# Three pairs of blocks chosen early in a kernel of attention, mixture of experts and feed-forward

## The chip, the cores and the metric

One NeuronCore of a Trainium2 chip runs the whole computation in one launch. The metric is the device time of one execution in microseconds (us); a kernel's time is the median of its runs. Profiles are of one execution, on the same core.

## The reference

```python
def reference(q, k, v, w_gate, w1, w2, w_in, w_out, alpha):       # cut to what matters
    # attention in chunks of 64: q, k, v are (8, 8, 576, 64)
    s = matmul(q_c, k_c.T) / 8
    p = exp(s - max(s)); p /= sum(p) + 1e-9
    x = matmul(p, v_c)                        # tokens x features: 4608 x 512
    # mixture of experts: 8 experts, each token goes to its best one
    logits = x @ w_gate                       # 4608 x 8
    e = argmax(logits); g = softmax(logits)[e]
    y[e == i] = g * (relu(x[e == i] @ w1[i]) @ w2[i])     # 512 -> 1024 -> 512
    # feed-forward: 512 -> 2048 -> 512
    h = y @ w_in
    return (max(h, 0) + alpha * min(h, 0)) @ w_out
```

`w_in` and `w_out` arrive as 64-bit numbers. Every product of the experts and of the feed-forward is made of three products of rounded parts (high x high, high x low, low x high).

## The kernel before, in words

**Attention and routing** goes over 36 tiles of 128 tokens. `STEP` is a hand-written order: in step s each named piece runs for the tile that lies its lag behind. Every few tiles `choose`, `rank` and `count` decide the expert of each token and its place among that expert's tokens; `place` writes the token's number into a table (PSUM tile `tb`) with one column for each block of 128 tokens of an expert. After 24 tiles (`TE`), `choose_early` takes the expert that has most tokens, and `begin_first` (L1029) copies the table and gathers this expert's first 384 tokens (`gather_first`), so that a first group of three tiles can go through its expert (`lead_up`, `lead_act`, `lead_down`) while the routing of the last tiles ends. `TAIL` is the written order of this change-over. In it, `slots` computes on DVE from the final counts which block each of 24 slots takes (16 pairs of 128-token blocks, 8 single blocks), where each result row goes (`yidx`) and the expert of each slot (`bx`); `end_table` copies the finished table, and `gather0` has POOL gather the first slot's rows by indirect DMA. `add_slots` hands the slots' experts to `Stream`, which loads expert weights in pieces of 512 KB on SP's queue (L428, L431), two ahead; each piece is split into a rounded part `whi` on ACT (L443) and the rest `wlo` (L451) on DVE, every fourth on POOL.

**Experts and feed-forward** run side by side (`experts_and_ffn`). The feed-forward goes over 12 groups of 384 tokens, each in 16 blocks f: an `fh` product (L340 to L342), `leaky` on DVE (L1206, L1207), the split of the result, an `fo` product (L385 to L387). The experts' work is 160 steps: 8 for each pair slot, 4 for each single slot; a step k is `slot_up` (`mh`), `act` (`mact`), its split and `slot_down` of the step before (`mo`). When a slot's last step is reached, the next slot's rows are turned (`take`: four transposes, into the bank `tr` and, for the second tile, into `mh`, which `act` must have read), the slot after is gathered on POOL, and in the step that follows `slot_out` scales the two accumulators on ACT (`row`), copies the row numbers on POOL and scatters the rows into `y_sorted` by an indirect DMA on POOL. Groups of the feed-forward read `y_sorted` in order, four blocks before they begin.

A planner (`due`, `pace`, `target`) says how many steps lie beside each block: straight lines through corners, of which the first is (block 1, 0 steps), the second (16, `FRONT`), and the others say when a group's rows must exist (`surely_done`). The order of the pieces within a block and its first step is `STEP2` in group 0, `STEP4` after it, `STEP3` for single slots; further steps of the same block (in group 0) run only the list's expert entries and its `("conv", "too")` entries.

**The conversion** of `w_in` and `w_out` from 64 bits (`Float64Weights`, L186 to L283) has 32 pieces; 12 are done beside the attention, 20 beside group 0, four ticks each: `bits` and `round` (L243, L244 on DVE, L254 on ACT, L255 on POOL), `square` (L261, ACT), `mask` (L269, DVE), `finish` (L282 on ACT, L283 on POOL). They share one buffer `word`. STEP2 has four ticks, two of them "too".

All of it is one order written out by hand: each engine takes its instructions in program order.

## Time and profile before

| | us |
|---|---|
| median of three runs (lowest, highest) | 1544.39 (1543.96, 1548.34) |
| the profiled execution | 1545.0 |
| its span, first to last instruction | 1543.2 |
| PE busy (matmuls) | 1475.8 |
| DVE / ACT / POOL busy | 834.1 / 660.8 / 451.9 |
| mean granted TensorE clock | 0.989 |

The span is the time between the first and the last instruction of the profiled execution; 1.8 us lie around it. PE is busy 96% of it, so a change is worth what it takes from the other 4%, from the stretches at the lower clock, or from PE's work. A share of the whole span hides where these are; the rows further down are therefore by stage.

### The profile page before, as it was taken

To read this page: it belongs to the slowest core of one execution; us is meant where nothing else is said; L and a number is where in the kernel's file an instruction comes from. 1 tells how busy PE (TensorE), PEld (TensorE's weight loads), DVE (VectorE), ACT (ScalarE), POOL (GpSimd) and SP (SyncE) were. 2 spreads that over 40 slices of the span, in tenths; PEclk is the share of its full clock that TensorE was granted. 3 is DMA by queue.
4 is the path that set the end of the run, shared out by engine and by line. 5 is a ranking of instruction groups with operands and counts; after the bars stand their busy time and mean duration, and the time that the engine had idled before them with its cause. 6 is when DMAs were issued, how large, how long until landed. Compare 5 with 4: busy or idle time off the path is not lost.

```text
span 1543.2 us, 25420 instructions
## 1 busy us (share of the span) xinstructions
PE 1475.8 (96%) x9736; PEld 1313.8 (85%) x9736; DVE 834.1 (54%) x1485; ACT 660.8 (43%) x1365; POOL 451.9 (29%) x428
## 2 busy tenths in 40 slices
PE   7887879988999999999999999999999999999998
PEld 5665768878899999999999999999989998999887
DVE  5688868776444444444444444444445555555343
ACT  6887446555423333333333333334334444344211
POOL 2256546666212212221232222212204223231100
PEclk9999899999999999999999999999999999999999
DMA  9998335555323323332342333233324544454000
GB/s 288 321 314 272 104 110 171 172 190 170 103 83 119 97 85 106 100 97 92 105 126 85 100 93 113 84 101 103 92 87 158 152 156 149 143 165 139 28 21 21
DMA packets 119128, 201.23 MB, mean 130 GB/s; under 512 B 12704, under 2 KB 63904, under 8 KB 119008
## 3 DMA queue, kind: packets, MB, share of 16 engines
q1 hardware_dynamic: 108112, 168.32, 35.1%
q0 software_dynamic: 10896, 31.31, 5.9%
q8 instruction: 76, 1.25, 0.3%
q14 instruction: 44, 0.36, 0.1%
HBM read 170.13 MB, written 29.46 MB: 129 GB/s over the span
## 4 chain that ended last, share of the span: by engine, by line
PE 77%; DVE 8%; DMA 6%; POOL 3%; issue 3%; ACT 1%; SPq 0%; POOLq 0%; another core or an unknown queue 0%; ACTq 0%; DVEq 0%
PE fh L340 8%; PE fh L342 8%; PE fh L341 8%; PE fo L385 8%; PE fo L386 8%; PE fo L387 8%; PE mh L342 3%; PE mh L341 3%; PE mh L340 3%; PE mo L385 3%; PE mo L387 3%; PE mo L386 3%; DMA kbd<-in_kh 2%; DVE word L269 2%; PE tr L304 2%
## 5 line engine op out<-in xcount | busy, mean ns | idle before, releaser
L451 DVE TENSOR_TENSOR wlo<-raw,whi 128x1024 fp32r<-128x1024 f32 x146 | 182.3, 1253 | 169.2 <-ACT whi L443 166.2
L340 PE MATMUL fh<-fxh,w 128*128 128x384 f32 x760 | 257.1, 338 | 6.1 <-DVE fact L1207 4.7
L443 ACT CAST whi<-raw 128x1024 fp32r<-128x1024 f32 x200 | 208.7, 1049 | 119.5 <-PE mo L387 49.7
L342 PE MATMUL fh<-fxh,w 128*128 128x384 f32 x760 | 257.0, 338 | 0.0
L341 PE MATMUL fh<-fxl,w 128*128 128x384 f32 x760 | 256.2, 337 | 0.3 <-issue 0.3
L451 POOL TENSOR_TENSOR wlo<-raw,whi 128x1024 fp32r<-128x1024 f32 x54 | 129.8, 2403 | 431.1 <-ACT whi L443 430.7
L1206 DVE TENSOR_SCALAR fact<-fh,alpha 128x384 f32<-128x384 f32 x190 | 116.9, 615 | 234.2 <-PE fh L342 226.9
L385 PE MATMUL fo<-w,fgh 128*128 128x512 f32 x567 | 225.1, 397 | 0.0
L386 PE MATMUL fo<-w,fgh 128*128 128x512 f32 x567 | 222.7, 393 | 0.0
L387 PE MATMUL fo<-w,fgl 128*128 128x512 f32 x567 | 221.8, 391 | 0.0
L1139 ACT ACTIVATE mact<-mh 128x256 f32<-128x256 f32 x160 | 61.2, 382 | 288.6 <-PE mh L342 287.0
L321 ACT CAST fgh<-fact 128x384 fp32r<-128x384 f32 x197 | 100.9, 512 | 180.8 <-DVE fact L1207 180.5
L340 PEld LDWEIGHTS fh<-fxh,w 128*128 128x128 f32 x760 | 143.5, 189 | 15.0 <-DVE fact L1207 5.6
L341 PEld LDWEIGHTS fh<-fxl,w 128*128 128x128 f32 x760 | 143.3, 189 | 8.2 <-issue 0.5
L342 PE MATMUL mh<-mxh,wlo 128*128 128x256 f32 x512 | 144.6, 282 | 0.0
L341 PE MATMUL mh<-mxl,whi 128*128 128x256 f32 x512 | 144.4, 282 | 0.0
L340 PE MATMUL mh<-mxh,whi 128*128 128x256 f32 x512 | 144.1, 282 | 0.0
L342 PEld LDWEIGHTS fh<-fxh,w 128*128 128x128 f32 x760 | 143.2, 188 | 0.0
L327 DVE TENSOR_TENSOR fgl<-fact,fgh 128x384 fp32r<-128x384 f32 x197 | 114.0, 579 | 35.6 <-ACT fgh L321 35.3
L327 DVE TENSOR_TENSOR mgl<-mact,mgh 128x256 fp32r<-128x256 f32 x128 | 63.0, 492 | 121.2 <-ACT mgh L321 121.2
L387 PEld LDWEIGHTS fo<-w,fgl 128*128 128x128 f32 x567 | 106.5, 188 | 23.4
L385 PEld LDWEIGHTS fo<-w,fgh 128*128 128x128 f32 x567 | 107.0, 189 | 17.5 <-ACT orow L1199 0.2
(231 smaller groups left out, 2702.8 us busy)
## 6 DMA issues: line engine op xcount, KB each, us to landing
raw<-in_w SPq DMA_DIRECT2D x200, 512.0 KB
vt<-in_vh SPq DMA_DIRECT2D x18, 520.0 KB
qt<-in_qh SPq DMA_DIRECT2D x18, 512.0 KB
kbd<-in_kh SPq DMA_DIRECT2D x36, 256.0 KB
x_tok<-x SPq DMA_DIRECT2D x36, 256.0 KB
x<-y_sorted SPq DMA_DIRECT2D x33, 258.0 KB
raw<-in_w_in SPq DMA_DIRECT2D x16, 512.0 KB
raw<-in_w_out SPq DMA_DIRECT2D x16, 512.0 KB
```

The source lines that it names most:

```text
L321: self.nc.scalar.copy(gh, self.g[key])
L327: self.nc.vector.tensor_sub(gl, t, gh.bitcast(F32))
L340: nc.tensor.matmul(b, wh[:, c, :], hi[:, c, :], start=(c == 0), stop=False)
L341: nc.tensor.matmul(b, wh[:, c, :], lo[:, c, :], start=False, stop=False)
L342: nc.tensor.matmul(b, wl[:, c, :], hi[:, c, :], start=False, stop=(c == 3))
L385: nc.tensor.matmul(o, gh[:, s], wh, start=first, stop=False)
L386: nc.tensor.matmul(o, gh[:, s], wl, start=False, stop=False)
L387: nc.tensor.matmul(o, gl[:, s], wh, start=False, stop=last)
L443: self.nc.scalar.copy(hi, raw)
L451: (engine or (self.nc.gpsimd if n % 4 == 3 else self.nc.vector)).tensor_sub(lo, raw, hi.bitcast(F32))
L1139: nc.scalar.activation(t, b, AF.Relu)
L1206: nc.vector.tensor_scalar(t, b, 0.0, s_.alpha[:, f:f + 1], op0=ALU.min, op1=ALU.mult)
```

## The change

- After 24 tiles `choose_pairs` computes on DVE, from the counts so far, three pairs of full blocks (256 tokens of one expert each; `NE` = 3), besides the early group: 18 small instructions, a prefix sum over the experts' full pairs among them. They become slots 0 to 2. `slots` deals out the rest only (`NL` = 21 slots).
- `gather0` moves from the end of `TAIL` to its beginning; the experts of the three pairs are given to `Stream` in `begin_first`, so that its loads go on without a stop, and `add_slots` has none to start.
- The rows of slots 0 to 2 have known places: `slot_out` writes them with a plain DMA on SP's queue instead of a scatter on POOL.
- `FRONT` rises from 30 to 40.
- In `STEP2` the second transpose comes after `down` instead of after the first, both `out` stand together, the gather and `take_low` move; in `STEP4` one entry moves.
- The pools of the second part, and the two PSUM pools of the lead group, are opened with `reuse_waits="tile"`: a tile waits for what lay in its own place, and not for all that lay in the place of its pool.
- The conversion loads its 13th piece at the start of the second part, no longer in the attention.

```diff
-FRONT = 30
+NE = 3
+NL = NS - NE
+AHEAD = GW + NE * PAIR
+FRONT = 40
 STEP2 = (
...
-    ("moe", "take", 0), ("moe", "take", 1), ("ffn", "in_high", 0), ("ffn", "high", 0), ("ffn", "in", 1),
-    ("moe", "act", 0), ("moe", "take_high", 0), ("moe", "down", 0), ("ffn", "in_low", 0), ("moe", "gather", 0),
-    ("moe", "out", 0), ("ffn", "in", 2), ("ffn", "low", 0), ("conv", "too", 0), ("ffn", "in_high", 1),
-    ("moe", "take_low", 0), ("moe", "high", 0), ("moe", "low", 0), ("moe", "split_high", 0), ("ffn", "in_high", 2),
-    ("conv", "", 0), ("conv", "too", 0), ("ffn", "down", 0), ("moe", "out", 1), ("ffn", "out", 2),
-    ("moe", "split_low", 0), ("moe", "take_high", 1), ("moe", "take_low", 1), ("ffn", "in_low", 2),
+    ("moe", "take", 0), ("ffn", "in_high", 0), ("ffn", "high", 0), ("ffn", "in", 1),
+    ("moe", "act", 0), ("moe", "take_high", 0), ("moe", "down", 0), ("moe", "take", 1), ("ffn", "in_low", 0),
+    ("moe", "out", 0), ("moe", "out", 1), ("ffn", "in", 2), ("moe", "take_high", 1), ("moe", "gather", 0),
+    ("moe", "take_low", 0), ("moe", "take_low", 1), ("ffn", "low", 0), ("conv", "too", 0), ("ffn", "in_high", 1),
+    ("moe", "high", 0), ("moe", "low", 0), ("moe", "split_high", 0), ("ffn", "in_high", 2),
+    ("conv", "", 0), ("conv", "too", 0), ("ffn", "down", 0), ("ffn", "out", 2),
+    ("moe", "split_low", 0), ("ffn", "in_low", 2),
...
 TAIL = (
     ("sum_logits", 30), ("transpose_x", 32), ("split_high", 0), ("gate", 27), ("weigh", 34), ("keep_x", 32),
+    ("gather0", 0),
...
-    ("place", 34), ("place", 35), ("down", 6), ("end_table", 0), ("low", 7), ("gather0", 0), ("down", 7), ("scale", 0),
+    ("place", 34), ("place", 35), ("down", 6), ("end_table", 0), ("low", 7), ("down", 7), ("scale", 0),
...
+    def choose_pairs(t1):
+        cnt = run[t1].rearrange("p a e -> p (a e)")
+        left, fi = small.tile([P, E], I32, tag="left", name="left"), small.tile([P, E], I32, tag="fi", name="fi")
+        nc.vector.scalar_tensor_tensor(left, early_oh, -float(GW), cnt, op0=ALU.mult, op1=ALU.add)
+        nc.vector.tensor_single_scalar(fi, left, 8, op=ALU.arith_shift_right)
...
+        nc.vector.tensor_copy(s_.pairs, val)
+        nc.vector.scalar_tensor_tensor(early_col, early_n, 2.0, early_col, op0=ALU.mult, op1=ALU.add)
...
     def more_psum(_):
         att.close()
-        lead.ps_h = ctx.enter_context(tc.tile_pool(name="ps_h1", bufs=1, space=PSUM))
-        lead.ps_o = ctx.enter_context(tc.tile_pool(name="ps_o1", bufs=1, space=PSUM))
+        own = dict(bufs=1, space=PSUM, reuse_waits="tile")
+        lead.ps_h = ctx.enter_context(tc.tile_pool(name="ps_h1", **own))
+        lead.ps_o = ctx.enter_context(tc.tile_pool(name="ps_o1", **own))
...
         gather_first()
+        choose_pairs(TE)
+        for a in range(NE):
+            stream.add(s_.pairs[a:a + 1, 1:2])
...
     def add_slots(_):
-        for i in range(NS):
+        for i in range(NL):
             stream.add(s_.bx[0:1, 1, i:i + 1])
-        for _ in range(RAWS):
-            stream.load()
...
-                        if stage == "mask" and s + 3 > NT:
+                        if stage == "bits" and s + 3 >= NT:
                             conv.leave()
...
-    conv.hold(ctx.enter_context(tc.tile_pool(name="c_held", bufs=1)))
-    two = ctx.enter_context(tc.tile_pool(name="c_two", bufs=2))
-    ps_m = ctx.enter_context(tc.tile_pool(name="ps_m", bufs=1, space=PSUM))
-    ps_f = ctx.enter_context(tc.tile_pool(name="ps_f", bufs=1, space=PSUM))
+    conv.hold(ctx.enter_context(tc.tile_pool(name="c_held", bufs=1, reuse_waits="tile")))
+    two = ctx.enter_context(tc.tile_pool(name="c_two", bufs=2, reuse_waits="tile"))
+    ps_m = ctx.enter_context(tc.tile_pool(name="ps_m", bufs=1, space=PSUM, reuse_waits="tile"))
+    ps_f = ctx.enter_context(tc.tile_pool(name="ps_f", bufs=1, space=PSUM, reuse_waits="tile"))
...
-        nc.gpsimd.indirect_dma_start(
-            out=y_sorted, out_offset=bass.IndirectOffsetOnAxis(ap=s_.yidx[:, a, i:i + 1], axis=0),
-            in_=row, in_offset=None,
-        )
+        if a < NE:
+            r = GW + a * PAIR + i * P
+            nc.sync.dma_start(y_sorted[r:r + P, :], row)
+        else:
+            nc.gpsimd.indirect_dma_start(
+                out=y_sorted, out_offset=bass.IndirectOffsetOnAxis(ap=s_.yidx[:, a - NE, i:i + 1], axis=0),
+                in_=row, in_offset=None,
+            )
```

## Rows read from the trace of the kernel before

**Rows 1.** Windows by stage: stretch, length, busy us per engine (count), PEclk, DMA share, GB/s.
```profile
218.00:375.00 157.00, 140.83 (x777) 124.69 (x778) 117.22 (x156) 93.00 (x166) 99.27 (x74) 0.96 0.54 177
375.00:1470.00 1095.00, 1092.43 (x6161) 993.86 (x6159) 528.60 (x809) 411.17 (x725) 251.73 (x254) 1.00 0.35 110
```

**Rows 2.** Waits of PE, 217 to 400 us: in total, times, longest.
```profile
PE tr L304 <- ACT mact L1139: 8.5, 3, 2.9
PE mo L385 <- ACT row L1166: 3.3, 3, 1.2
```

**Rows 3.** Timeline, DVE: start, us, engine, line, operation, tiles, count, [idle before <- releaser].
```profile
296.08 0.43 DVE L243 TENSOR_SCALAR word<-raw 128x512 int32<-128x512 int32 x1
...
302.10 0.43 DVE L243 TENSOR_SCALAR word<-raw 128x512 int32<-128x512 int32 x1 [1.20 <-POOL w L283]
```

**Rows 4.** Timeline, first `bits` and last subtraction of the 20 pieces.
```profile
222.65 0.42 DVE L243 TENSOR_SCALAR word<-raw 128x512 int32<-128x512 int32 x1
...
372.93 1.35 POOL L283 TENSOR_TENSOR w<-word,w 128x512 fp32r<-128x512 f32 x1
```

**Rows 5.** Timeline around the gather of a slot: POOL and ACT.
```profile
266.26 0.18 POOL L496 COPY ix<-table 128x2 int32 x1
...
267.07 0.62 ACT L282 CAST w<-word 128x512 fp32r<-128x512 f32 x1 [0.35 <-DVE word L269]
...
272.44 1.31 POOL L283 TENSOR_TENSOR w<-word,w 128x512 fp32r<-128x512 f32 x1
```

**Rows 6.** Timeline, the same DVE link alone and beside a weight split on POOL.
```profile
266.35 0.69 DVE L269 SCALAR_TENSOR_TENSOR word<-raw,word 128x512 f32<-128x512 f32 x1 [1.19 <-POOL word L255]
...
284.05 2.41 POOL L451 TENSOR_TENSOR wlo<-raw,whi 128x1024 fp32r<-128x1024 f32 x1
...
284.13 2.88 DVE L269 SCALAR_TENSOR_TENSOR word<-raw,word 128x512 f32<-128x512 f32 x1 [1.05 <-POOL word L255]
```

**Rows 7.** Timeline of PE: starts of one block's `fo`, a step, `fh`, the next step.
```profile
227.97 0.40 PE L385 MATMUL fo<-w,fgh 128*128 128x512 f32 x1
...
230.04 0.28 PE L340 MATMUL mh<-mxh,whi 128*128 128x256 f32 x1
...
232.86 0.33 PE L340 MATMUL fh<-fxh,w 128*128 128x384 f32 x1
...
234.96 0.28 PE L340 MATMUL mh<-mxh,whi 128*128 128x256 f32 x1
```

**Rows 8.** Timeline around the second scatter of a slot: DVE and POOL.
```profile
280.25 0.69 DVE L244 SCALAR_TENSOR_TENSOR word<-raw,word 128x512 int32<-128x512 int32 x1
...
281.75 1.01 POOL L1168 DMA_INDIRECT y_sorted<-row,yidx  x1 [1.86 <-ACT raw L261]
```

**Rows 9.** Timeline of the change-over to group 0: ACT and PE.
```profile
211.46 2.05 ACT L1072 ACTIVATE x<-fo,gfirst 128x512 f32<-128x512 f32 x3 [1.99 <-PE fo L387]
...
213.56 0.66 PE L304 MATMUL fi<-ident,x 128*128 128x128 f32 x4 [0.78 <-ACT x L1072]
...
217.82 0.44 PE L340 MATMUL fh<-fxh,w 128*128 128x384 f32 x1 [1.40 <-ACT fxh L308]
```

**Rows 10.** Timeline, DVE: one small instruction of `slots`.
```profile
190.46 0.17 DVE L923 SCALAR_TENSOR_TENSOR sl_single<-sl_over,sl_single 128x8 f32<-128x8 f32 x1
```

**Rows 11.** Timeline, DVE, the end of the attention.
```profile
153.93 0.17 DVE L712 TENSOR_SCALAR den<-av 128x8 f32<-128x8 f32 x1 [2.66 <-remote]
```

**Rows 12.** Timeline: the first weight split on POOL, PE's first product with it.
```profile
160.93 2.40 POOL L451 TENSOR_TENSOR wlo<-raw,whi 128x1024 fp32r<-128x1024 f32 x1
...
169.95 0.53 PE L340 MATMUL fh<-fxh,whi 128*128 128x384 f32 x1
```

**Rows 13.** Timeline, PE: second block of group 1.
```profile
400.59 0.44 PE L340 MATMUL fh<-fxh,w 128*128 128x384 f32 x1 [1.30 <-DVE fact L1207]
```

**Rows 14.** Timeline, DVE and POOL, of another piece.
```profile
289.24 0.41 DVE L243 TENSOR_SCALAR word<-raw 128x512 int32<-128x512 int32 x1
...
290.62 2.09 POOL L255 TENSOR_TENSOR word<-word,raw 128x512 int32<-128x512 int32 x1 [1.57 <-DVE word L244]
```

More of the change, by code (lines that the diff above doesn't have):

```diff
@@ L135, in surely_done @@
 def surely_done(n):
-    low = N
-    for full in range((N - GW) // PAIR + 1):
-        rest = N - GW - full * PAIR
+    if n <= NE:
+        return GW + n * PAIR
+    low, n, pairs = N, n - NE, NP - NE
+    for full in range((N - AHEAD) // PAIR + 1):
+        rest = N - AHEAD - full * PAIR
         for part in range(E + 1):
@@ L143, in surely_done @@
                     continue
-                over = max(0, full + part - NP)
-                m = min(max(min(n, NP) - full, 0), part - over)
+                over = max(0, full + part - pairs)
+                m = min(max(min(n, pairs) - full, 0), part - over)
                 done = PAIR * min(n, full)
@@ L148, in surely_done @@
                     done += max((P + 1) * m, rest - (PAIR - 1) * (part - m) - P * single)
-                if n >= NP:
-                    done = max(done, N - GW - P * max(0, single + 2 * over - (n - NP)))
-                low = min(low, GW + done)
+                if n >= pairs:
+                    done = max(done, N - AHEAD - P * max(0, single + 2 * over - (n - pairs)))
+                low = min(low, AHEAD + done)
     return low
@@ L483, with __init__ @@
 class Gather:
-    def __init__(self, nc, pool, table, slots, x_tok, g_tok):
-        self.nc, self.pool, self.table, self.slots, self.x_tok, self.g_tok = nc, pool, table, slots, x_tok, g_tok
+    def __init__(self, nc, pool, table, early, slots, x_tok, g_tok):
+        self.nc, self.pool, self.table, self.early, self.slots = nc, pool, table, early, slots
+        self.x_tok, self.g_tok = x_tok, g_tok
         self.xs, self.gs, self.rows = {}, {}, {}
@@ L493, in __call__ @@
         nc, n = self.nc, tiles_of(a)
-        r = nc.gpsimd.value_load(self.slots[0:1, 0, a:a + 1], min_val=0, max_val=NCODE - 2)
+        first = self.early[a:a + 1, 0:1] if a < NE else self.slots[0:1, 0, a - NE:a - NE + 1]
+        x_tok, g_tok = ((y[:TE * P] if a < NE else y) for y in (self.x_tok, self.g_tok))
+        r = nc.gpsimd.value_load(first, min_val=0, max_val=NCODE - 2)
         ix = self.pool.tile([P, 2], I32, tag="ix", name="ix", bufs=4)
@@ L501, in __call__ @@
             nc.gpsimd.indirect_dma_start(
-                out=x, out_offset=None, in_=self.x_tok,
+                out=x, out_offset=None, in_=x_tok,
                 in_offset=bass.IndirectOffsetOnAxis(ap=ix[:, i:i + 1], axis=0),
@@ L541, in tile_attention_moe_ffn @@
     s.table = const.tile([P, NCODE], I32, name="table")
-    s.yidx = const.tile([P, NS, 2], I32, name="yidx")
-    s.bx = const.tile([P, 2, NS], I32, name="bx")
+    s.yidx = const.tile([P, NL, 2], I32, name="yidx")
+    s.bx = const.tile([P, 2, NL], I32, name="bx")
     s.first = const.tile([P, GT], I32, name="first")
-    s.gather = Gather(nc, share, s.table, s.bx, s.x_tok, s.g_tok)
+    s.pairs = const.tile([P, 2], I32, name="pairs")
+    s.gather = Gather(nc, share, s.table, s.pairs, s.bx, s.x_tok, s.g_tok)
     s.early_i = const.tile([P, 2], I32, name="early_i")
@@ L638, in attention_and_routing @@
     nc.vector.tensor_scalar_mul(kmaxe, iota_f[:, :E], float(KMAX))
-    oneE = one.tile([P, NS], F32, name="oneE")
+    oneE = one.tile([P, NL], F32, name="oneE")
     nc.vector.memset(oneE, 1.0)
@@ L652, in attention_and_routing @@
     early_oh = one.tile([P, E], F32, name="early_oh")
+    early_n = one.tile([P, E], F32, name="early_n")
+    early_col = one.tile([P, E], F32, name="early_col")
     tb = ps_tb.tile([P, NCODE], F32, name="tb")
@@ L900, in slots @@
         ci, fi, ri = new([E], "ci", I32), new([E], "fi", I32), new([E], "ri", I32)
-        nc.vector.scalar_tensor_tensor(ci, early_oh, -float(GW), cnt, op0=ALU.mult, op1=ALU.add)
+        left = new([E], "left")
+        nc.vector.scalar_tensor_tensor(left, early_oh, -float(GW), cnt, op0=ALU.mult, op1=ALU.add)
+        nc.vector.scalar_tensor_tensor(ci, early_n, -float(PAIR), left, op0=ALU.mult, op1=ALU.add)
         nc.vector.tensor_single_scalar(fi, ci, 8, op=ALU.arith_shift_right)
@@ L917, in slots @@
         over = new([E], "over")
-        nc.vector.scalar_tensor_tensor(over, lo[:, 1], float(NP), part, op0=ALU.is_ge, op1=ALU.mult)
+        nc.vector.scalar_tensor_tensor(over, lo[:, 1], float(NP - NE), part, op0=ALU.is_ge, op1=ALU.mult)
         nc.vector.tensor_add(hi[:, 1], lo[:, 1], part)
@@ L1310, in experts_and_ffn @@
     ctx.enter_context(convs)
-    conv.use(convs.enter_context(tc.tile_pool(name="c_conv", bufs=1)), 2)
+    conv.use(convs.enter_context(tc.tile_pool(name="c_conv", bufs=1, reuse_waits="tile")), 2)
     first = dict(
```

46 lines of the change are left out of this document (32 added, 14 removed).

## The prediction

> **What bounds the kernel now.** I read the windows by stage first: where is TensorE idle? In 375 to 1470 us it works 1092 of 1095 us at full clock [rows 1], so work moved out of there is worth its own length and nothing more. Idle time lies in the attention, in the change-over after it and in 218 to 375, where the first group of the second layer runs beside the conversion of the last 20 of its 32 weight pieces: there PE is busy 140.8 of 157 us at a mean granted clock of 0.96, so 16.2 us idle, and 2 x 0.04 x 157 = 12.6 us at 1.2 instead of 2.4 GHz, worth 6.3 us.
>
> The waits of PE in that stage name the obvious suspect: the second transpose of a slot's rows waits three times, 8.5 us in all, for `mact`, and the first product of a new slot 3.3 us for the copy of the old accumulators [rows 2]. The reorder of STEP2 is about just these.
>
> But a wait of PE is worth its length only if PE is what ends last there. So the third view is the chain of one converted piece over DVE, ACT and POOL: `bits` (L243) starts at 296.08, and the next piece's at 302.10, having waited 1.20 us for the last subtraction of the piece before on POOL (L283) [rows 3]. The one buffer `word` makes the pieces strictly serial, 6.0 us each when nothing intervenes. The first starts at 222.65, the 20th ends at 372.93 + 1.35 = 374.28 [rows 4]: 151.6 us, back to back. 20 x 6.0 is 120; the rest is what POOL does between two links: a slot's gather holds it from 266.26 until L283 can start at 272.44, though ACT's link before that ended at 267.07 + 0.62 = 267.69, 4.7 us (three times, 14) [rows 5]; a weight split on POOL makes the next DVE link 2.88 instead of 0.69 us (six times, 13) [rows 6]; and the scatters come on top. **The conversion chain, not PE, sets the length of this stage**; PE's waits are where its slack shows.
>
> **The change, part by part.** Part 1, *40 steps instead of 30 beside group 0*. The planner's first corner moves from 30 to 40 steps at block 16; no later due is steeper, so the rest still runs to 137 steps at block 139 and 161 at 171. Blocks 1 to 15 now take 2, 3, 3 steps in turn instead of 2. Each block ticks the conversion 4 times and each step beyond its first twice more, as before. The 80 ticks (20 pieces x 4) end in the first pass of block 13 before, and after in that of block 11 (4 in block 0, then 6 + 8 + 8 in turn: 76 after block 10). What PE gets done by then: a step is 232.86 - 230.04 = 2.82 us, an `fh` 234.96 - 232.86 = 2.10, an `fo` 230.04 - 227.97 = 2.07 [rows 7]. Before: 2.1 + 13 x 4.17 + 25 x 2.82 + 3 slots' transposes of 1.0 = 129.8. After: 2.1 + 11 x 4.17 + 27 x 2.82 + 3.0 = 127.1. So if the chain's length stays, **2.7 us more** PE work is left when it ends. The ten steps themselves cost nothing: they leave a stage where PE is full. Ranges: 0 to +4.
>
> Part 2, *scatters of the first three slots from POOL to SP*. The second scatter of a slot starts at 281.75, after 1.86 us of waiting, and keeps POOL until 282.76; the chain's next POOL link had its input from L244's end at 280.94 and would start some 0.2 us later [rows 8]: 1.6 us lost. The second slot shows the same, the third scatters when the conversion is over: together **-3.2 us** of the chain. On SP the row copies stand behind nothing of the chain; queued behind them are the next weight loads, which are there a piece ahead, so I put them at 0, up to +1 per slot if they come late. Range -3.2 to +2.
>
> Part 3, *transposes and copies in another order*. By the waits it is worth 8.5 + 3.3 us and their share of the clock; in a stage set by the chain it is worth **0**, if no link of the chain waits for these PE instructions. The only one that could is the gather, which reuses the transposed rows' buffers: POOL goes into it at 266.26 straight from work, with no idle time named [rows 5]. What is late next is the chain.
>
> Part 4, *waits by tile instead of by pool*. Of three `scale` copies (211.46 to 213.51) the first transpose needs only the first, but starts at 213.56, after the third, and group 0 at 217.82 [rows 9]; the accumulators lie in pools that it must see emptied as a whole. By tile it starts when PE is done with `fo`, about 212.8; then ACT's five casts of 0.59 us follow `scale` without a hole (213.5 + 5 x 0.59 = 216.4) and group 0 starts there: **-1.4 us**; range -1.4 to 0.
>
> Part 5, *choosing the pairs, and gather0 early*. 18 small DVE instructions at 0.17 us, as one of their kind in `slots` [rows 10]: 3.1 us, at about 146 to 150 us. There DVE stands still for 2.66 us shortly after [rows 11], waiting for PE; what held PE the rows don't show. If that wait is tied to a time, it covers 2.7 of the 3.1; if to PE's own place in its order, nothing. gather0 holds POOL some 6.2 us as in [rows 5], ahead of the first weight split, which ran from 160.93 for 2.40 us; PE's first product with it is at 169.95 [rows 12]. Put back by the whole 6.2 the split ends at 169.5: covered, barely. The split's place also decides which DVE instruction it blocks, for 2.2 us either way [rows 6]. A conversion piece of 512 KB is no longer loaded there. Ends: -2.2, and 3.1 + 2.2 = +5.3; I take **+1.0**, toward the covered end, as DVE's idle row is the nearest. After the change gather0 no longer follows the table at the end of the change-over, but no wait there names it [rows 9].
>
> Part 6, *the steps' new rhythm later*. A group whose first block has no step waits 1.30 us for `fact` [rows 13], as group 1 does, and group 11 like it. By the new slope group 6 also begins with no step: **+1.3**. `slots` changes by single small instructions: 0.
>
> Sum: +2.7 - 3.2 + 0 - 1.4 + 1.0 + 1.3 = **+0.4 us**. The profiled execution took 1545.0 us (span 1543.2), the median of the runs is 1544.39; the difference applied to the median is **1544.8**. The parts' ends, not all at once, give 1538 to 1550 for this case.
>
> **A rule weighed.** When POOL's `wlo` starts at 284.05, the DVE link that starts at 284.13 takes 2.88 instead of 0.69 us [rows 6]. The Trainium skill's page "SBUF — State Buffer", section "SBUF: two separate sides", says why: the port pair that DVE and GpSimd share is an exclusive lock held for a whole instruction, so that the other fully blocks. The trace agrees: the split takes 2.41 of those 2.88. By this rule the two engines' idle shares are no room for ten steps; were they independent, PE's idle time could be filled and the sum would be rival A's. In the windows DVE and POOL together are busy 117.2 + 99.3 us in 157 [rows 1], stalls included.
>
> **Rivals.** *A: PE's waits are a loss of their own.* Then 8.5 + 3.3 us go, and three quarters of the clock's 6.3 (one of four falls at the stage's start): 16.5, less about 1 us that each of now five slots may still wait, plus parts 4 to 6 (+0.9): -10.6, **1534**. For it: PE waits just there. Against: the 20 pieces stand back to back, and their length is told by DVE's and POOL's own work.
> *B: the chain gets longer.* With three steps in a row, splits and copies of two steps lie between pairs of ticks. The piece whose `bits` is at 289.24, with POOL's add drawn out to 2.09 us, already takes until 296.08, 6.8 instead of 6.0 us [rows 3, 14]. If twelve of 20 pieces become such, 12 x 0.8 = 9.6, on top of the +0.4: **1554**. It decides against the kernel where the mean of an undisturbed piece passes 6.4 us. For it: DVE and POOL share the stage's work with little room. Against: there are hardly more steps to a tick, 8 to 22 against 2 to 6.
> *C: choose_pairs and gather0 aren't covered*: part 5 at its upper end, 4.3 more than taken, **1549**, at the edge of what counts as no change.
>
> **How the numbers follow.** About 0.3% (4.6 us) is what a measurement of this kernel can tell from no change. Forecast 0.42, A 0.29, B 0.20, C 0.09. Same: the forecast less its fringes of 0.03 and 0.01, and over half of C, 0.43; faster: A and the fringe, 0.32; slower: B, the rest of C and the fringe, 0.25. Cases of both signs hold much: the range reaches into both, **1532 to 1554**; the forecast's own is 1538 to 1550.
>
> **What would show it.** The `tr` waits on `mact` shrink in the profile after; if the stage from 218 us to the end of the 20th piece is nevertheless 147 to 149 us long, with PE idle near 20, part 3 is right at 0. No `y_sorted` on POOL before the fourth slot; the first `fi` before 213 us less the attention's shift; one more 1.3 us wait on `fact` near group 6. I am wrong if pieces no longer follow each other without gaps (then PE sets the stage, A), or if their mean rises (B).

## The result: 1560.0 us, slower by one per cent

The changed kernel takes 1560.03 us (median of five runs, 1557.19 to 1565.92) against 1544.39; the ratio is 1.010, 95% interval 1.0078 to 1.0123. A second series of the same program gave 1560.01 (1.0078 to 1.0122). Forecast were 1544.8, 1532 to 1554: the time lies above the range. The profiled execution took 1557.75 us, its span is 1555.9 (before: 1543.2).

The windows by stage, as in [rows 1], first the change-over, then group 0 with the conversion (columns: stretch, its length, busy us and count per engine, PEclk, DMA share, GB/s):

```profile
145.00:155.00 10.00, 5.44 (x50) 4.54 (x50) 7.46 (x36) 4.98 (x14) 8.11 (x9) 0.66 0.63 210
155.00:165.00 10.00, 5.01 (x97) 3.52 (x98) 5.30 (x13) 2.41 (x5) 7.76 (x8) 0.99 0.42 130
165.00:175.00 10.00, 6.12 (x32) 4.44 (x32) 8.40 (x23) 3.65 (x7) 3.97 (x4) 0.50 0.36 109
...
218.00:375.00 157.00, 138.43 (x774) 118.16 (x775) 119.19 (x156) 96.73 (x172) 99.42 (x72) 0.99 0.55 182
```

Group 0 looks as forecast: PE is idle 18.6 of 157 us (16.2 in [rows 1]), at a clock of 0.99 instead of 0.96. The change-over from 145 to 175 us does not: PE works 16.6 of 30 us (before 19.7), and at 1.2 GHz through all of the third line. PE's waits show the same, and a third place (line waited for, us in total, times, longest). First the change-over, 143 to 222 us, then group 0 (218 to 435), then all behind it:

```profile
PE bx L741 <- DVE lg_all L783: 3.8, 1, 3.8
PE lgt L777 <- DVE rk L839: 3.7, 1, 3.7
...
PE mo L394 <- ACT mgh L330: 5.1, 5, 1.9
PE mo L396 <- DVE mgl L336: 4.8, 12, 0.8
PE mh L349 <- ACT mact L1185: 4.0, 7, 1.5
...
PE mo L395 <- POOL wlo L460: 1.6, 3, 0.5
...
PE fh L349 <- DVE fact L1257: 3.2, 3, 1.3
PE tr L313 <- DVE fxl L321: 2.5, 1, 2.5
```

The waits of `tr` on `mact` (8.5 us) and of `mo` on `row` (3.3 us) of [rows 2] are gone. In their place PE waits some 15 us for `mgh`, `mgl`, `mact` and `wlo` (with 30 steps in the new order, 5.8 for `mgh` alone), and behind group 0 there is a new wait of 2.5 us, of `tr` on `fxl`.

To see where the time goes, I cut each trace at marks that every version has: the end of attention's last score products; ACT's first `scale` copy (`x<-fo,gfirst`, 211.46 in [rows 9]); the first `fact` of group 0; the first `bits` and the last subtraction of the 20 conversion pieces (222.65 and 374.28, [rows 4]); the first `fact` of group 1; the end. In the changed kernel:

```profile
140.35 1.09 PE L679 MATMUL s<-kbd,qt 128*64 128x128 f32 x16
...
214.45 2.06 ACT L1118 ACTIVATE x<-fo,gfirst 128x512 f32<-128x512 f32 x3 [1.99 <-PE fo L396]
...
222.38 0.62 DVE L1256 TENSOR_SCALAR fact<-fh,alpha 128x384 f32<-128x384 f32 x1
...
223.50 0.42 DVE L252 TENSOR_SCALAR word<-raw 128x512 int32<-128x512 int32 x1
...
373.66 1.56 POOL L292 TENSOR_TENSOR w<-word,w 128x512 fp32r<-128x512 f32 x1 [1.62 <-ACT w L291]
...
432.80 0.61 DVE L1256 TENSOR_SCALAR fact<-fh,alpha 128x384 f32<-128x384 f32 x1
```

| us | before | changed | difference |
|---|---|---|---|
| start to the end of the last scores | 143.6 | 141.4 | -2.1 |
| scores to first `scale` (change-over) | 67.9 | 73.0 | +5.1 |
| `scale` to group 0's first `fact` | 10.1 | 7.9 | -2.1 |
| `fact` to the first `bits` | 1.1 | 1.1 | 0 |
| chain of 20 pieces | 151.6 | 151.7 | +0.1 |
| last piece to group 1's first `fact` | 25.0 | 57.6 | +32.6 |
| group 1 to the end | 1143.9 | 1123.1 | -20.8 |
| span | 1543.2 | 1555.9 | +12.7 |

Ten steps of 2.82 us and two slots' transposes (0.9 each) are 30.0 us that the plan moves from the line "group 1 to the end" to the one above it; without them these two lines are +2.6 and +9.2. The lines behind the first `scale` repeat within 0.3 us from trace to trace of one program, but for one stretch at half clock that may or may not fall at the conversion's end (25.0 or 23.5 us with 30 steps in the new order). The first two lines do not repeat (141 to 147, and 64 to 74 us). So the stretch from the first `scale` to the end is the sharpest measure here: **1331.8 before, 1341.5 after, +9.7**, and the change-over adds about 5.

### The profile page after: what moved, and what is told of

The parts are those of the page before. It is cut to its first block, busy times and chain, and to the rows that moved or that the text cites. A ratio compares the mean times of both kernels' runs of the same rounds, so it can differ in the third digit from the quotient of the medians.

```text
span 1555.9 us, 25436 instructions
## 1 busy us (share of the span) xinstructions
PE 1483.7 (95%) x9736; PEld 1316.5 (85%) x9736; DVE 836.2 (54%) x1503; ACT 661.5 (43%) x1365; POOL 443.2 (28%) x422
```

## The experiments

Theory: the loss behind the conversion comes from where the new plan puts the change of slots, the rest from the change-over; rival: from one place alone. The table has all versions but e2 and e3; each ratio is against runs of the kernel before in the same series. The four columns of stretches are from the profiled execution, the last is from all runs.

| run | edit | scores to `scale` | chain | group 1 to end | `scale` to end | median, ratio (95% interval) |
|---|---|---|---|---|---|---|
| before | | 67.9 | 151.6 | 1143.9 | 1331.8 | 1544.39 |
| changed | | 73.0 | 151.7 | 1123.1 | 1341.5 | 1560.03, 1.010 (1.0078 to 1.0123) |
| e9 | the same again | 72.9 | 151.5 | 1123.1 | 1341.2 | 1560.01, 1.010 (1.0078 to 1.0122) |
| e1 | 30 steps | 73.0 | 147.9 | 1143.4 | 1325.3 | 1546.83, 0.9994 (0.9976 to 1.0011) |
| e10 | the same again | 73.9 | 147.9 | 1143.5 | 1323.9 | 1545.80, 0.9999 (0.9986 to 1.0011) |
| e4 | before, tile waits only | 67.3 | 151.3 | 1143.3 | 1331.4 | 1545.79, 0.9998 (0.9977 to 1.0019) |
| e5 | 38 steps, slot change moved | 65.6 | 154.2 | 1122.0 | 1334.2 | 1546.67, 1.0004 (0.9988 to 1.0021) |
| e14 | 40 steps, one slot change moved | 72.9 | 152.4 | 1120.6 | 1339.6 | 1557.23, 1.0082 (1.0062 to 1.0102) |
| e8 | 30 steps, old order | 64.4 | 147.8 | 1143.9 | 1325.8 | 1539.46, 0.9951 (0.9933 to 0.9970) |
| e13 | the same again | 72.4 | 147.9 | 1143.8 | 1325.7 | 1544.45, 0.9987 (0.9974 to 1.0001) |
| e15 | 38 steps, old order | 73.0 | 160.5 | 1122.5 | 1340.6 | 1561.63, 1.0098 (1.0081 to 1.0115) |
| e11 | 30 steps, scatters by POOL | 72.9 | 161.2 | 1143.4 | 1334.7 | 1557.18, 1.0069 (1.0053 to 1.0084) |
| e6 | 30 steps, gather0 late | 68.2 | 147.8 | 1143.5 | 1326.3 | 1541.57, 0.9970 (0.9955 to 0.9985) |
| e7 | 30 steps, choose_pairs late | 68.6 | 147.8 | 1143.4 | 1325.2 | 1543.61, 0.9975 (0.9958 to 0.9991) |
| e12 | 30 steps, both late | 70.0 | 147.9 | 1143.3 | 1324.8 | 1545.53, 0.9991 (0.9979 to 1.0003) |
| e16 | e7 with the old order | 70.7 | 147.8 | 1143.4 | 1325.3 | 1543.17, 0.9979 (0.9965 to 0.9993) |

**e1, e9, e10: the number of steps.** In e1 and e10 one number of the changed kernel is undone:

```diff
-FRONT = 40
+FRONT = 30
```

> The changed kernel with 30 steps beside group 0 again; all else (early gather0 and choose_pairs, row copies by SP, STEP2 and STEP4 in the new order, waits by tile) stays. Theory T (most of the loss comes from where the 40 steps put the later slot changes and empty blocks: 8 us behind the conversion, 2.6 in group 0; the start costs 0.9 net): 1544.4 + 0.9, and up to 3 less if PE's waits for mact in group 0 go without denser steps in their place: 1542 to 1546. Rival R (the loss arises in the change-over and in SP's row copies, which are still here): 1555 or more. In its profile T wants no wait of tr on fxl over 2 us and no half clock behind 400 us; group 1 begins within 3 us of 399.3.

> The changed kernel as it is, beside the 30-step version and the kernel before on one chip. From the first scale copy of the change-over to the end its trace took 1341.4 us, the kernel before 1331.7, the 30-step version 1325.3; ahead of that copy the traces differ from one execution to the next (attention's last scores at 141 to 147 us). Theory T: the stretch behind the first scale copy is again 1341 within 1, 9 to 10 more than before; the whole 1557 to 1561. Rival R (the change-over's early part is what the change lost): the stretch behind is within 4 us of before's.

> The 30-step version once more, on the same chip as the changed kernel itself. Theory T: 16 us faster than the changed kernel (1341.4 - 1325.3 behind the first scale copy), the same ahead of it: 1541 to 1545, and a little faster than the kernel before. Rival R2 (the early choose_pairs and gather0 put the change-over into a slower rhythm for good, as in the first run of this version: first product of the first layer at 174 us, half clock for 13.7 us from 165): again 1546 to 1548, first product at 174 or later.

Measured: behind the first `scale` 1325.3 and 1323.9 instead of 1341.5 and 1341.2. That is 16 to 17 us for ten steps, as theory T expected, and the medians of one series (e9, e10) differ by 14.2. It is the whole net loss: with 30 steps the kernel is level with the one before (3.8 less in the chain and 2.1 less at group 0's start, against 5 more in the change-over). Of the 16.2, group 0 has 6.4 (chain 3.8 longer, 2.6 more PE work left behind it) and the rest has 9.7 (1123.1 - 1143.4 + 30.0). The medians of e1 and e10 lie 0.8 above the ranges of theory T (e1's rival R is out by 8): the change-over took its 73 us again, which R2 had expected.

**e2, e3: misbuilt.** They were to move one slot change by another due point, but the point was put behind the last due, which the planner takes as the end; 33 steps then fell into the last block of group 7.

```diff
+    due.append((NF * NP // 2 - 1, FP * NP))
     pace = [due[0]]
```

> The changed kernel with 38 steps beside group 0 and one more due point, 128 steps by block 127, so that slot 15 ends in block 14 of group 7 and no slot changes in the last block of a group; only groups 0 and 1 begin with an empty block. Theory T: the changed kernel's 1560.0 less 4.4 (group 7: wait on fxl and the half clock behind it), 1.2 (empty first block of group 6) and 1.4 (half clock after group 0's last block): 1553, range 1551 to 1555. Rival R (start and group 0 are all of it): 1559 to 1561.

> The changed kernel with 40 steps as it is, and only the due point of 128 steps by block 127 added. The slot change in group 7's last block goes, that in group 0's last block stays, and groups 4 and 7 begin with an empty block instead of group 6. Theory T: 1560.0 - 4.4 + 1.3 = 1556.9, range 1555 to 1558.5, with no tr wait on fxl near 1163 us and no half clock there. Rival R: unchanged, 1559 to 1561.

Measured: 1668.47 and 1673.48 us. They decide nothing about the slot change; e5 and e14 are the same edits done rightly.

**e5, e14: the slot change in a group's last block.** With 40 steps, slot 4 ends in the last block of group 0, and slot 15 in the last block of group 7. There the next group's rows are turned as well, through the same bank `tr`. With 30 steps no slot ends in a last block. The timeline of the changed kernel at group 7's end:

```profile
1160.66 0.60 PE L313 MATMUL tr<-ident,x 128*128 128x128 f32 x4
1161.30 0.58 ACT L317 CAST fxh<-tr 128x512 fp32r<-128x512 f32 x1 [2.92 <-PE tr L313]
...
1162.20 0.40 ACT L330 CAST mgh<-mact 128x256 fp32r<-128x256 f32 x1
1162.64 0.42 DVE L336 TENSOR_TENSOR mgl<-mact,mgh 128x256 fp32r<-128x256 f32 x1 [1.88 <-ACT mgh L330]
1162.98 0.68 DVE L321 TENSOR_TENSOR fxl<-tr,fxh 128x512 fp32r<-128x512 f32 x1
...
1163.72 0.44 PE L313 MATMUL tr<-ident,xg 128*128 128x128 f32 x2 [2.46 <-DVE fxl L321]
```

The transposes of one tile of the group are done at 1161.26; their bank is free when DVE has taken `fxl` out of it, but DVE stands first at `mgl`, which waits for ACT's `mgh`, queued behind two other pieces. PE waits 2.46 us for the slot's transposes, and from 1165.0 on it runs 3.4 us at 1.2 GHz. In e14 only a due point is added (in e5 also `FRONT = 38`, so that no slot ends in a last block at all):

```diff
+    due.insert(next(i for i, d in enumerate(due) if d[0] == NF * NP // 2 + NF - 5), (NF * NP // 2 - 1, FP * NP))
     pace = [due[0]]
```

> The changed kernel with 38 steps beside group 0 and a due point of 128 steps by block 127 put in its place in the list of dues (in the run named e2 it stood last, where the planner takes it for the end). No slot then changes in the last block of a group, and only groups 0 and 1 begin with an empty block. Theory T (a slot change in the last block of a group, and an empty first block, cost what the trace showed: 4.4 in group 7, 1.2 in group 6, 1.5 at the end of group 0; denser steps in group 0 cost 6.4 against 30 steps, four fifths of it here): the 30-step run's 1546.8 + 5.1 + 2.6 = 1554.5, range 1552 to 1556. Rival (the slot change is paid wherever it falls, the loss belongs to the denser front alone): 1559 to 1561.

> The changed kernel with one edit: the due point of 128 steps by block 127, in its place in the list. Slot 15 then ends in block 14 of group 7 and not in its last block; the slot change in group 0's last block stays; empty first blocks in groups 4 and 7 instead of group 6. Theory T: behind the first scale copy 1341.4 - 4.4 + 1.2 = 1338.2, range 1337 to 1339.5, and group 7 without the 2.5 us wait of tr on fxl and without the half clock. Rival (the wait for the slot change moves along to block 14): 1341 to 1342.

The windows of the same 20 us, the changed kernel, then e14:

```profile
1150.00:1170.00 20.00, 17.54 (x95) 15.54 (x94) 7.33 (x12) 5.11 (x10) 4.11 (x7) 0.91 0.19 66
...
1150.00:1170.00 20.00, 20.00 (x115) 17.95 (x114) 10.87 (x17) 8.25 (x15) 2.60 (x6) 1.00 0.31 92
```

PE idle 2.46 us and the clock of 0.91 are gone. Group 7 of the changed kernel takes 110.1 us (first `fact` to first `fact`); e1's 108.1 less one step (2.82) and with four transposes more (0.4) is 105.7, so 4.4 are lost there. In e14, with one step less still, the same sum leaves 1.6, of which 1.3 is PE's wait for `fact` in the group's empty first block. From `scale` to end the whole gains 1.9, just outside the range: the chain was 0.7 longer, and group 1 to the end gained 2.5 where 3.2 were expected. The rival (1341 to 1342) is out.

In e5, where nothing ends in a last block, group 1 to the end is 1122.0; 1143.4 less eight steps and one slot's transposes (23.5) is 1119.9, so 2.1 are left of the 9.7, and 1.4 of these are one wait of PE for `mgh` in group 8, where the single slots begin. **The slot changes in last blocks and the empty first block are 7.6 us.** The groups agree. The changed kernel's group 1, which runs 3.4 us at half clock just behind the slot change in group 0's last block, takes 105.6 us, e5's 105.0 with as many steps and one slot's transposes (0.9) more: 1.5. Group 6, with the empty first block, takes 105.0, e5's 106.2 with a step more: 1.6. Group 7, with as many steps, takes 110.1 against 105.8: 4.3. The rival (the loss is that of the denser front alone) is out. e5's median was 1546.7, below both expectations (1554.5; 1559 to 1561), with a change-over of 65.6 us in its trace; from `scale` to end it is 1334.2, against 1325.3 + 7.7 = 1333.0 expected.

**e8, e13, e15: the order of STEP2 and STEP4.** Both lists are put back to those of the kernel before, in the 30-step version (e8, e13) and in e5 (e15):

```diff
-    ("moe", "act", 0), ("moe", "take_high", 0), ("moe", "down", 0), ("moe", "take", 1), ("ffn", "in_low", 0),
-    ("moe", "out", 0), ("moe", "out", 1), ("ffn", "in", 2), ("moe", "take_high", 1), ("moe", "gather", 0),
+    ("moe", "take", 0), ("moe", "take", 1), ("ffn", "in_high", 0), ("ffn", "high", 0), ("ffn", "in", 1),
+    ("moe", "act", 0), ("moe", "take_high", 0), ("moe", "down", 0), ("ffn", "in_low", 0), ("moe", "gather", 0),
...
```

> The 30-step version with STEP2 and STEP4 in the order of the kernel before (part 3 undone). Theory T (the conversion chain sets group 0): the waits of tr on mact come back, 8 us of them, and the time stays: 1546.8 within 1.5, 20 pieces 148 us long. Rival A (PE's waits are a loss of their own): 1555 or more. A third: the reorder itself cost the chain, then it shortens and the time falls below 1545.

> The 30-step version with the old orders once more. Up to the first product of the first layer its program is the 30-step version's, instruction for instruction; yet the stretch from attention's last scores to that product took 21.8 us in its trace and 32.5 in three traces with the new orders (30 or 40 steps). Theory P (which of the two lengths comes is fixed by the program as a whole, by when PE gets its next instructions): again about 22, 1538 to 1541 in all. Theory J (it changes from load to load): anything from 22 to 33, and the time 1539 to 1549 with it. Behind the first scale copy both expect 1325.8 within 1.

> The version with 38 steps and no slot change in a last block, with STEP2 and STEP4 in the old order. With the new orders the stretch behind the first scale copy was 1334.2 and the chain 154.2. Theory T (the chain sets group 0 with dense steps too): 1334 within 1.5, though the waits of tr on mact come back, some 10 us of them in five slots. Rival A (with dense steps PE has no slack left, and the new order is what makes them bearable): 1338 to 1345. Third: the new order put more POOL work between the links, then the chain is below 152 and the stretch 1330 to 1333.

PE's waits from 218 to 375 us, with 30 steps, the new order (e1), then the old one (e13):

```profile
PE mo L394 <- ACT mgh L330: 5.8, 3, 1.9
PE tr L313 <- ACT mact L1185: 2.5, 3, 0.8
...
PE tr L312 <- ACT mact L1184: 7.6, 3, 2.9
PE mo L393 <- ACT row L1211: 3.5, 3, 1.3
```

The old order brings 11 us of waits back for 8 that go, and group 0 takes 174.0 us in both (172.5 in e10, where no stretch at half clock falls at the chain's end): with 30 steps the order is worth nothing, 1.5 us at most, as in part 3. With 38 steps it is worth 6.4 us (1340.6 against 1334.2; rival A's range), and all of it is in the chain, 160.5 against 154.2, most of it in one piece, the thirteenth: 12.2 us against 7.0. e15 shows how a wait of PE gets into the chain: DVE's `mask` of that piece, then ACT, then PE:

```profile
324.94 0.69 DVE L277 SCALAR_TENSOR_TENSOR word<-raw,word 128x512 f32<-128x512 f32 x1 [0.41 <-POOL word L263]
...
327.61 0.38 ACT L1184 ACTIVATE mact<-mh 128x256 f32<-128x256 f32 x1 [3.80 <-PE mh L350]
...
331.11 0.61 ACT L290 CAST w<-word 128x512 fp32r<-128x512 f32 x1
...
324.58 0.58 PE L348 MATMUL mh<-mxh,whi 128*128 128x256 f32 x1 [3.25 <-DVE mxl L320]
```

The piece's rounding on ACT (L290) has its input at 325.63, but starts at 331.11: in ACT's order it stands behind `mact`, which waited 3.80 us for PE's `mh`, which had waited 3.25 us for `mxl`. (The old orders with 40 steps were not run, so what the order is worth there is not known.)

**e11: who writes the rows.** The row copies of slots 0 to 2 are scattered by POOL again, to the same rows:

```diff
-        if a < NE:
-            r = GW + a * PAIR + i * P
-            nc.sync.dma_start(y_sorted[r:r + P, :], row)
-        else:
+        if True:
             nc.gpsimd.indirect_dma_start(
-                out=y_sorted, out_offset=bass.IndirectOffsetOnAxis(ap=s_.yidx[:, a - NE, i:i + 1], axis=0),
+                out=y_sorted, out_offset=bass.IndirectOffsetOnAxis(
+                    ap=s_.prow[:, 2 * a + i:2 * a + i + 1] if a < NE else s_.yidx[:, a - NE, i:i + 1], axis=0),
```

> The 30-step version with the row copies of the first three slots issued as scatters by POOL again, to the same rows (part 2 undone). Theory T: the chain of 20 pieces goes from 148.0 back to 151.6, and the time with it: 3.6 more than the 30-step version of the same call. Rival: the scatters had been hidden and the gain came from the new order: chain 148, same time.

Measured: the chain grows by 13.3 us, which neither theory expected (3.6 and 0), and the time by 11 (e10, same series). POOL in e11:

```profile
282.08 1.18 POOL L1217 DMA_INDIRECT y_sorted<-row,prow  x1 [0.28 <-POOL row L1215]
...
286.72 0.99 POOL L1217 DMA_INDIRECT y_sorted<-row,prow  x1 [3.18 <-DMA y_sorted<-row,prow]
287.73 1.29 POOL L292 TENSOR_TENSOR w<-word,w 128x512 fp32r<-128x512 f32 x1
```

The second scatter waits 3.18 us for the first to land, and in the new order the two `out` stand side by side, so that POOL has nothing else to do meanwhile; the subtraction (L292) starts 5.3 us after the start of the ACT link it follows, instead of 0.7. In the old order the second scatter waited 1.86 us [rows 8], with the chain's subtraction done meanwhile, and there the edit gave 3.8 (151.6 before, 147.8 in e8; waits by tile alone leave 151.3, e4). So part 2 was right for the order it was read from, and the two parts need each other.

**e4: waits by tile alone.** In the kernel before, the pools are opened with `reuse_waits="tile"`.

```diff
-    two = ctx.enter_context(tc.tile_pool(name="c_two", bufs=2))
+    two = ctx.enter_context(tc.tile_pool(name="c_two", bufs=2, reuse_waits="tile"))
...
```

> The kernel before with nothing but the waits of the pools by tile (part 4 alone). Theory T: the step held, 1.4 to 1.8 us off the start of group 0, and the conversion chain hands them on: 1542.6 to 1543.2. Rival: the start moves, but the conversion's first piece does not, so nothing at the end: 1544.4. Second rival: the new waits let PE or ACT run into work it had been kept from, and the whole is longer: above 1546.

Measured: no difference, 0.9998 (0.9977 to 1.0019), as the first rival has it, and `scale` to `fact` took 10.6 us, not 10.1. PE in e4 (`scale` starts at 212.47):

```profile
213.63 0.60 PE L304 MATMUL fi<-ident,x 128*128 128x128 f32 x4
...
216.00 0.66 PE L304 MATMUL tr<-ident,xg 128*128 128x128 f32 x4 [0.87 <-DMA xg<-x_tok,ix]
...
218.80 0.45 PE L340 MATMUL fh<-fxh,w 128*128 128x384 f32 x1 [1.27 <-ACT fxh L308]
```

The first transposes do move, from 2.10 to 1.16 us behind the start of `scale`, as part 4 says. But then PE stands 0.87 us for the rows (`xg`) that the late `gather0` brings, and group 0's first `fh` starts 6.33 us behind `scale`, as before (6.36 [rows 9]); the rest of the 10.6 holds a stretch at half clock. In the changed kernel, where the rows are there early, that `fh` starts 4.5 us behind `scale`. So these waits alone bring nothing, and with the early rows 1.8 of the 2.1 us.

**e6, e7, e12, e16: the change-over.** e6 puts `gather0` back; e7 moves `choose_pairs` into a wait of DVE and `gather0` behind the second weight split; e12 moves `choose_pairs` and puts `gather0` back; e16 is e7 with the old orders. The edit of e7:

```diff
-    ("gather0", 0),
-    ("transpose_x", 33), ("logits", 31), ("keep_p_v", 35), ("normalise", 34), ("keep_logits", 31), ("weigh", 35),
+    ("transpose_x", 33), ("logits", 31), ("keep_p_v", 35), ("late_pairs", 0), ("normalise", 34), ("keep_logits", 31), ("weigh", 35),
...
-    ("take_low", 2), ("more_psum", 0), ("keep_logits", 35), ("up", 0), ("rank_in_tile", 31), ("split_low_p", 1),
+    ("take_low", 2), ("more_psum", 0), ("keep_logits", 35), ("up", 0), ("rank_in_tile", 31), ("split_low_p", 1), ("gather0", 0),
```

> The 30-step version of the changed kernel with gather0 back at its old place at the end of the change-over. Theory T: from the first scale copy to group 0's first fact it is 7.9 us with the early gather and 10.0 without (10.6 with tile waits alone), so the early gather is what gained there: +2.1, 1549. Rival: the 2.1 come from another edit (the rows are not what group 0 waits for): 1546.8, and 7.9 us stay. The first product of the first layer stays near 174 us under both, as choose_pairs is still ahead of it; a third reading, that gather0 on POOL is what delayed that product from 170 to 174, wants it back at 170.

> The 30-step version with the 18 instructions of choose_pairs moved into DVE's wait ahead of the normalisation of tile 34 (DVE stood still for 4.4 us there), and gather0 behind the second weight split. Theory T: choose_pairs cost the change-over some 4 us of which nothing was covered, because PE's next product needed DVE; moved, the first product of the first layer starts near 170 again and the whole takes 1543, range 1541 to 1545. Rival (that start is set by POOL or by the half clock, which the waits ahead of it cause in any order): 1546 to 1548.

> The 30-step version with choose_pairs moved into DVE's wait ahead of the normalisation of tile 34 and gather0 back at its old place. Theory T: the first product of the first layer as early as in the kernel before (167 to 170 us), behind the first scale copy 1326 us, the whole 1538 to 1541 and so faster than the kernel before. Rival (the order in the change-over makes no steady difference): as the 30-step version of the same call, within 1.5.

> A candidate: 30 steps, old orders, row copies of three slots by SP, waits by tile, choose_pairs in DVE's wait ahead of the normalisation of tile 34, gather0 behind the second weight split. Theory T: behind the first scale copy 1325.5; PE's wait of 3.7 us for rk is back at 0.6, the first product 28 us after attention's last scores as with the new order, or 19 if the 22 of the old order and the moved 3.1 add: 1536 to 1544, faster than the kernel before. Rival: no steady gain in the change-over, 1545 to 1547.

PE's waits from 143 to 222 us: the kernel before, e6, e16.

```profile
PE av L702 <- issue: 4.9, 2, 3.3
...
PE lgt L776 <- DVE rk L838: 3.7, 1, 3.7
...
PE tr L312 <- DMA xg<-x_tok,ix: 1.0, 2, 0.8
...
PE av L715 <- issue: 4.3, 2, 2.7
...
PE lgt L775 <- DVE rk L837: 0.6, 1, 0.6
```

`choose_pairs` adds 3.1 us to PE's wait for `rk` (3.7 against 0.6), the 18 x 0.17 of part 5. Yet e6, with `choose_pairs` in its place, takes 68.2 us from scores to `scale`, e7, with it moved, 68.6, and the kernel before 67.9: in the total its price does not show. (The kernel before and e16 stand 4.9 and 4.3 us at `av` with nothing that the trace shows to release PE, named "issue"; e6 and e7 do not.)

Does the early `gather0` cost the rest? With it, and `choose_pairs` in place, the change-over takes 72.4 to 73.9 us in eight of the table's ten traces, and the two weight splits on POOL hold up two DVE instructions there. But the two others, e5 and e8, take 65.6 and 64.4, less than any trace with the gather late (67.3 to 70.7); and with the gather late the splits of e6 hold up the same two instructions, which take 0.34 and 0.19 us by themselves:

```profile
163.43 2.41 DVE L866 TENSOR_SCALAR lo<-iota_f,lf_all,rid 128x128 fp32r<-128x128 f32 x1
...
166.76 2.33 DVE L799 TENSOR_TENSOR oh<-ra,first 128x32 bf16<-128x32 f32 x1
```

So the price of `gather0` is not shown either. What all eight long traces have, and e5 and e8 have not, is a wait of DVE of 4.3 to 4.4 us at `den<-av`, some 20.7 us behind the last scores. e13 is e8's program once more, in another series on another chip, and it took 72.4 (theory J). PE, DVE and POOL, first in e13 (last scores at 143.59), then in e8 (145.85):

```profile
160.05 0.70 PE L716 MATMUL av<-vt,pt 64*64 64x65 f32 x32 [0.77 <-DVE x L729]
...
164.28 0.17 DVE L726 TENSOR_SCALAR den<-av 128x8 f32<-128x8 f32 x1 [4.37 <-remote]
...
165.65 2.15 DVE L866 TENSOR_SCALAR lo<-iota_f,lf_all,rid 128x128 fp32r<-128x128 f32 x1
...
168.73 2.34 DVE L799 TENSOR_TENSOR oh<-ra,first 128x32 bf16<-128x32 f32 x1
...
165.37 2.35 POOL L459 TENSOR_TENSOR wlo<-raw,whi 128x1024 fp32r<-128x1024 f32 x1
...
168.68 2.33 POOL L459 TENSOR_TENSOR wlo<-raw,whi 128x1024 fp32r<-128x1024 f32 x1
...
160.93 0.17 DVE L726 TENSOR_SCALAR den<-av 128x8 f32<-128x8 f32 x1 [1.01 <-PE av L716]
...
162.30 0.34 DVE L866 TENSOR_SCALAR lo<-iota_f,lf_all,rid 128x128 fp32r<-128x128 f32 x1
...
163.44 0.19 DVE L799 TENSOR_TENSOR oh<-ra,first 128x32 bf16<-128x32 f32 x1
...
166.52 2.35 POOL L459 TENSOR_TENSOR wlo<-raw,whi 128x1024 fp32r<-128x1024 f32 x1
```

In e8 `den` starts 0.2 us after PE's `av` has ended; in e13 3.5 us after it (160.75), and the trace does not name what released it ("remote"). DVE had stood 2.01 us in the same way 8 us earlier, and PE 1.51 us with no releaser in between. By `lo` e13 is 5.6 us later behind its last scores than e8 (22.1 and 16.5), before any split has held it up; then both instructions fall behind splits, and it is 9.7 by the end of `oh` and 8.0 at `scale`. PE's wait in e13:

```profile
PE av L716 <- issue: 1.9, 2, 1.5
```

So of e6's expectations none holds whole: the first product comes 26.8 us behind the last scores (26.4 before, 32.3 in the changed kernel), as the third reading wanted, but e5 and e8 have it at 21.5 with the gather early; and 1.0 us is lost again where group 0 waits for the rows (`tr` on `xg`; `scale` to `fact` 8.9 instead of 7.9), half of theory T's 2.1. e7 came out at theory T's numbers (1543.6; first product at 169.9), though not shown to be for T's reason, as e6 is as short. e12 is as its rival has it (1545.5, beside 1545.8 for e10), and e16's 1543.2 lies in theory T's wide range. No place of the two pieces gave a steady gain.

**What is faster than the kernel before.** e6 (30 steps, `gather0` late) takes 0.9970 of it (0.9955 to 0.9985), e16 0.9979 (0.9965 to 0.9993), e7 0.9975 (0.9958 to 0.9991), each in one series; e8's 0.9951 did not repeat (e13: 0.9987), so a series can be off by as much as these gain. Steady is what lies behind `scale`: 5.5 to 7.9 us less than before in every version with 30 steps and plain row copies, 3.8 of it in the chain and 1.1 to 2.1 between `scale` and group 0.

## Why the prediction was wrong, point by point

- **Part 1, the ten steps.** "The ten steps themselves cost nothing: they leave a stage where PE is full" is the step that failed. What they leave is full of PE work, and that much was right; but the new slope also moves the block in which each slot changes. Two changes now meet a group's turn of rows, and that with the empty block costs 7.6 of 9.7 us (e1, e5, e14). The prediction looked at the new rhythm only for empty first blocks (part 6).
- **Part 1, what is left when the chain ends**: +2.7 forecast, +2.6 measured (57.6 - 25.0 - 30.0), with a chain as long as before. Right.
- **"So if the chain's length stays".** It did not: 147.9 with 30 steps, 151.7 with 40, otherwise the same program. The pieces still follow each other without a gap (PE idle 18.6 us, as the stage set by the chain wanted), but their mean rose from 7.40 to 7.58 us: rival B's mechanism, at 3.8 of its 9.6 us. (The sign "147 to 149 us" fits the chain, 151.6 - 3.2, and not the stretch from 218 us that its sentence names; the chain measured 151.7.) It shows where splits meet links, POOL then DVE:

```profile
281.13 2.41 POOL L460 TENSOR_TENSOR wlo<-raw,whi 128x1024 fp32r<-128x1024 f32 x1
...
281.20 2.62 DVE L252 TENSOR_SCALAR word<-raw 128x512 int32<-128x512 int32 x1 [0.61 <-POOL w L292]
```

  `bits` takes 2.62 instead of 0.43 us here, as [rows 6] had it for `mask`; three such in the chain cost 6.5 us; two gathers between `bits` and the addition cost 6.6; the two POOL links themselves take 3.2 more; fewer gathers and splits behind the other links give 12.6 back. The rule that was weighed, from the Trainium skill's page "SBUF — State Buffer", section "SBUF: two separate sides" (whoever starts first, GpSimd or a DVE instruction with two SBUF inputs or in a 2-port mode, keeps the shared pair for its whole instruction), fits again in length: the split started 0.07 us earlier. `bits` has one input, and whether it runs in such a mode no trace here tells.
- **Part 2**: -3.2 forecast, -3.8 measured with the old order (e8 against before). Right. It was hidden from the total by the +3.8 above: against the kernel before, the chain did not change (151.6 and 151.7).
- **Part 3**: 0 forecast. Right with 30 steps (e1 and e13, 174.0 us of group 0 each), though the row of waits changes by 11 us. Wrong with 38: the new order saves 6.4 us there, through ACT's order (e15); with 40 it was not measured. "In a stage set by the chain it is worth 0" holds only as long as PE has slack.
- **Part 4**: -1.4 forecast; alone it is 0 (e4), because the next transposes then wait for the rows. With the early rows group 0's first `fh` comes 1.8 us earlier. Right in size, but it needs part 5's `gather0`, which the forecast set apart ("no wait there names it [rows 9]"; with the wait for the pools gone, e4 names it: 0.87).
- **Part 5**: +1.0 forecast, +5.1 measured in the change-over (67.9 and 73.0 us). That this is near its upper bound (+5.3) is luck: the terms of the bound, an uncovered `choose_pairs` (3.1) and one split that blocks a DVE instruction (2.2), are not what the traces show. `choose_pairs` has no price that shows (e6, e7), and splits block two DVE instructions in the kernel before, too (2.13 and 1.79 us). What the long traces share is DVE's late `den`; why it comes, and whether the early `gather0` brings it on, stays open.
- **Part 6**: +1.3 for group 6. Measured: PE waits 1.3 us there, and the group loses 1.6. Right, but the smaller part of what the rhythm does.

Rivals: A is out with 30 steps, where PE's waits for `mact` and `row` came and went and the time stayed; with 38 steps e15's 6.4 us are of its kind, and they were what the new order saved. B came at 3.8 of its 9.6 us, and C's 4.3 in size (4.1), not shown to be for its reason. The slot changes, which no case had, put the sum above the range. In the stretches of the first table: +2.6 and +9.2 behind the conversion, +0.1 in the chain, -2.1 at group 0's start, +5.1 in the change-over, -2.1 ahead of it: +12.7, where the forecast had +0.4.

What stays open: what makes DVE's `den` late in the change-over, and so whether that takes 65 or 73 us; and the 0.7 us of e5's remainder that no wait names.

## What to carry to other kernels

Where a planner spreads one stream of work beside another, work out for the old and the new slope in which block each rare event falls (a change of buffers, a turn of rows), and look for two that now meet: here that decided, and moving work between two full stages did not. Cut every trace at the same marks before comparing totals; here that separated 9.7 us that repeat within 0.3 from a stretch that differs by 8 us between two traces of one program. A wait off the bound costs nothing only while its engine has slack: undo such an edit at the old and at the new density before calling it free.

## What was not expected of the hardware

- One program, run in two series on two chips, took 64.4 and 72.4 us for the same change-over (e8, e13). The difference is 5.6 us before any DVE instruction is held up by POOL: DVE starts on a product 3.5 us after its row on PE has ended in e13, 0.2 us in e8. Whether chip or load decides was not tried.
- A scatter from POOL to a tensor waits for the one before it to land: 3.18 us when they stand side by side (e11). With other work between, the second had 1.86 us of wait left, for which the profile names ACT [rows 8].
- 18 new DVE instructions for which PE waited 3.1 us more did not show in the length of the change-over (68.2 us in e6, 67.9 before, 68.6 with them moved in e7).
